# Pooled attention before two mixture-of-experts layers: K loaded in runs of 96 rows, a reordered start, and a routing carry on GpSimd

## The chip, the core and the metric

The program runs on one core of a Trainium2 chip. The metric is device time of one execution, in microseconds (us). The engines: TensorE (PE) for matmuls and transposes, VectorE (DVE), ScalarE (ACT), GpSimd (POOL), and SyncE (SP), whose queue issues nearly all loads and stores. Each engine runs its own instructions in the order in which they are written; waits between engines are semaphores.

## What is computed

```python
def _attn_ref(q, k, v):                       # 8 batches, 8 heads, 576 rows, 64 wide
    k_p = k.reshape(B, H, Sp, 8, D).mean(axis=3)      # 576 rows pooled to 72
    v_p = v.reshape(B, H, Sp, 8, D).mean(axis=3)
    scores = scale * np.matmul(q, k_p.transpose(0, 1, 3, 2))
    attn = softmax(scores)
    return np.matmul(attn, v_p)

x = attention, as 4608 tokens of 512
x = moe(x, ...)      # 8 experts, 512 -> 1024 -> 512, the best expert by x @ w_gate + modality bias
x = moe2(x, ...)     # the same with a skip score, added to x
```

## The kernel before

**Columns and units.** The attention stage works in 36 columns of 128 query rows. Two batches make nine columns: a unit is 256 rows of one batch (two columns, even and odd rows), and a ninth column holds the last 64 rows of both batches. For column c the engines do, in the loop from line 562: `emit_S` (TensorE: the scores, L310, into one PSUM tile of two banks that each column uses again; VectorE: their maximum `mx`, L316), `emit_qT` for column c + 2 (TensorE transposes q, L289; ScalarE copies it, L293), `emit_eT` for column c - 1 (L357, L359), `emit_exp` (TensorE subtracts the maximum with a matmul on `mx`, L336; ScalarE takes the exponential, L340), and `emit_AV` for column c - 3 (L377). `after_AV` then lets VectorE divide (`rec`, `x`, L395 to L402) and form the routing logits `LG` (L406); ScalarE and SP finish and store the unit's tokens to `xd`. S(c) below means the L310 matmuls of column c.

**Supply.** `load_q` brings a unit of q, `split_q` copies it on ScalarE (L167) three or four columns ahead of use. K and V are summed over eight rows: V of a batch in two halves of three runs of 96 rows (`load_v`, `pool_v`), the first half on GpSimd as three additions (L181 to L183), the second on VectorE as three reductions (L176). K of the first two batches comes in runs of 126 rows (`load_kb`, `pool_kb`, `prep_kb`); K of the other six in four tiles of 108 pooled rows that cross batches, each in two halves of four heads, summed on GpSimd (`load_k`, `pool_k`), transposed by `prep_k` (L239, four transposes) and copied to `KB` by ScalarE (L244). The tables `pool_at` and `prep_at` say in which column each sum and each preparation is issued; `order` and `free_after` say in which column a load is issued, as soon as the buffer three loads back is free. Instructions of VectorE in `pool_at` and the V scale `VB` (L260) are put into the list `late` and issued right behind the next column's `mx`.

**Routing beside the columns.** At columns 12, 21 and 30 a generator `route` is put into a background queue for nine columns each; every `bg.tick()` issues one step, six ticks a column, `pace` times (2 from column 22). The steps: `rt_mx` (VectorE, L838), three steps on `rt_eq` (GpSimd for the first two groups, L840 to L844), `lag[0]` idle steps, `rt_my` (VectorE, L850), `M` and `rt_ms` (GpSimd), `lag[1]` idle steps, a running sum `rt_i` (VectorE, L867), the carry to the next group (L871), a matmul, and the ranks `BB` (L891 to L901). Behind it in the same queue stand 18 one-hot tables `OB` (`route_places`, GpSimd, L911) for each group, then the next group's `route`. `count` (L916) sums the carry over partitions from a bfloat16 copy `cb`.

Of the kernel before, what the change touches and what calls it, by code (L numbers as in the profile page):

```python
# [9 lines left out]
F32 = mybir.dt.float32  # L10
# [26 lines left out]
NB0 = 2  # L37
KT = (B - NB0) * SP // 4
TILES = [(NB0 * SP + KT * i, NB0 * SP + KT * i + KT) for i in range(4)]

KR = [(126 * i, min(126 * i + 126, H * SP)) for i in range(5)]
VC = 96


def segments(t):

    g0, end = TILES[t]
    g = g0
    while g < end:
        b, sp = divmod(g, SP)  # L50
        n = min(SP - sp, end - g)
        yield b, sp, sp + n, g - g0
        g += n


def attention(tc, g, q, k, v, mid, w_gate, bias, const, moe):
# [4 lines left out]
    with ExitStack() as ctx:  # L61
# [55 lines left out]
        def load_k(t, hf):  # L117
            a = raw.tile([128, 5, POOL * D], F32, tag="k", name="kt", bufs=3)[:, 0:4]
            for b, s0, s1, p0 in segments(t):
                for h in range(4):  # L120
                    nc.sync.dma_start(
                        out=a[p0:p0 + s1 - s0, h, :],
                        in_=k[b, 4 * hf + h, s0 * POOL:s1 * POOL, :].rearrange(
                            "(s r) d -> s (r d)", r=POOL),
                    )
            raw_t["k", t, hf] = a
# [68 lines left out]
        def pool_k(t, hf, eng):  # L195
            d = sums_of(("k", t), [KT, H, D])
            pool_rows(d[:, 4 * hf:4 * hf + 4, :], raw_t.pop(("k", t, hf))[0:KT], eng)

# [34 lines left out]
        def prep_k(t):  # L233
            bg.settle()
            n = KT
            ks = sum_t.pop(("k", t))
            ps = ps_m.tile([128, 4, 128], F32, tag="m", name="ps_k")
            for hp in range(4):
                nc.tensor.transpose(  # L239
                    ps[:, hp, 0:n], ks[:, 2 * hp:2 * hp + 2, :].rearrange("p h d -> p (h d)"),  # L240
                    g.ident[0:n, 0:n])
            for b, s0, s1, p0 in segments(t):
                for i in range(2):
                    nc.scalar.copy(  # L244
                        KB[b % NR][64 * i:64 * i + 64, :, SP * i + s0:SP * i + s1],
                        ps[64 * i:64 * i + 64, :, p0:p0 + s1 - s0])
# [176 lines left out]
        def idle():  # L423
            for _ in range(3):
# [5 lines left out]
        pool_at = {0: [(pool_kb, 1, 2, 4, P), (pool_kb, 1, 0, 2, V), (pool_kb, 1, 4, 5, V)],  # L430
                   1: [(pool_v, 1, 0, P)]}
# [5 lines left out]
        for b, cs in ((1, (3, 4, 4)), (2, (5, 6, 7)), (3, (10, 11, 12)), (4, (14, 15, 16)),  # L437
                      (5, (18, 19, 20)), (6, (20, 21, 22)), (7, (24, 25, 26))):
# [21 lines left out]
        kq += [((pool_k, t, hf), [(load_k, t, hf)]) for t in range(4) for hf in range(2)]  # L460
# [1635 lines left out]
```

## Time and profile before

| | us |
|---|---|
| median of 3 runs | 941.45 |
| lowest, highest | 939.84, 943.73 |
| the profiled execution | 939.02 |
| its span | 937.3 |
| TensorE busy in the span | 891.4 (95%) |
| VectorE, GpSimd, ScalarE busy | 703.4, 510.6, 368.0 |

Attention covers the first 200 us, beside which the first expert blocks begin at 185. A row of the timeline gives start, duration, engine, line, operation, tile written and read, and in brackets the idle time before it and what ended that. A row of the windows gives the stretch, then busy time (and instructions) of PE, PEld, DVE, ACT and POOL, the clock granted to TensorE (1.00 is 2.4 GHz, 0.50 is 1.2 GHz), the DMA engines' busy share and GB/s.

### The profile page before, as it was taken

Reading aid. Unit: us, or ns where it says so; the run is one execution under the profiler, and the core shown is the slowest. Engines: PE = TensorE matmul, PEld = TensorE weight load, DVE = VectorE, ACT = ScalarE, POOL = GpSimd, SP = SyncE. Lnnn points to the kernel's source line nnn. Section 1 sums busy time; section 2 is a strip of 40 time slices with the busy share of each in tenths; the row PEclk is TensorE's granted clock in tenths of the full one; section 3 lists DMA queues with packets and bytes.
Section 4 is the critical chain, followed back from the end, with each engine's and each line's share of the span. In section 5 each row is a group of like instructions: output and inputs, shape, how many; then the busy total and the mean of one; then the engine's idle time right before and its main releaser. Section 6 shows DMA issues by size and latency. Waiting matters only on the chain. (4 is left out here: it accounts for less than half of the span.)

```text
span 937.3 us, 19065 instructions
## 1 busy us (share of the span) xinstructions
PE 891.4 (95%) x6231; PEld 801.6 (86%) x6231; DVE 703.4 (75%) x1815; ACT 368.0 (39%) x727; POOL 510.6 (54%) x762
## 2 busy tenths in 40 slices
PE   8899989899999999998999979999999999999995
PEld 6799889888899999987999869999988988979983
DVE  5487787887778888889877898877665778687672
ACT  4466556552222222251222422213414556565551
POOL 5766597413246657665766557575653444445341
PEclk9799899999999999999999999999999999999997
DMA  9999965623222211442224521227125683661441
GB/s 235 220 251 254 259 195 170 194 71 113 69 68 84 74 40 56 148 149 67 81 83 132 174 79 64 75 74 252 57 68 160 208 249 104 224 225 36 133 141 44
DMA packets 86141, 126.07 MB, mean 135 GB/s; under 512 B 13192, under 2 KB 50104, under 8 KB 85866
## 3 DMA queue, kind: packets, MB, share of 16 engines
q1 hardware_dynamic: 75386, 96.68, 33.1%
q0 software_dynamic: 10608, 27.67, 9.7%
q8 instruction: 63, 1.03, 0.5%
q14 instruction: 84, 0.69, 0.3%
HBM read 182.09 MB, written 39.50 MB: 236 GB/s over the span
## 5 line engine op out<-in xcount | busy, mean ns | idle before, releaser
L1414 PE MATMUL ps_g<-xh,w1h 128*128 128x256 f32 x896 | 256.3, 286 | 3.8 <-DVE hl L1419 2.2
L1414 PE MATMUL ps_g<-xl,w1h 128*128 128x256 f32 x896 | 253.2, 283 | 2.2 <-DVE xl L1367 2.2
L1414 PE MATMUL ps_g<-xh,w1l 128*128 128x256 f32 x896 | 252.3, 282 | 0.0
L1744 DVE CUSTOM_DVE_ANT_0 hr<-x,W 128x512 bf16<-128x512 f32 x324 | 227.9, 703 | 19.1 <-DVEq L1343 6.3
L1463 PE MATMUL ps_g<-w2h,hh 128*128 128x512 f32 x464 | 190.5, 411 | 3.2 <-ACT w2h L1354 1.9
L1463 PE MATMUL ps_g<-w2h,hl 128*128 128x512 f32 x464 | 185.1, 399 | 7.0 <-DVE hl L1419 7.0
L1463 PE MATMUL ps_g<-w2l,hh 128*128 128x512 f32 x464 | 184.1, 397 | 0.0
L1414 PEld LDWEIGHTS ps_g<-xh,w1h 128*128 128x128 f32 x896 | 169.2, 189 | 8.4 <-DVE hl L1419 2.6
L1414 PEld LDWEIGHTS ps_g<-xl,w1h 128*128 128x128 f32 x896 | 168.8, 188 | 3.9 <-DVE xl L1367 3.0
L1414 PEld LDWEIGHTS ps_g<-xh,w1l 128*128 128x128 f32 x896 | 169.2, 189 | 0.0
L1418 ACT ACTIVATE hh<-ps_g 128x512 fp32r<-128x512 f32 (+1 forms) x116 | 67.7, 583 | 242.5 <-PE ps_g L1414 240.3
L1419 DVE SCALAR_TENSOR_TENSOR hl<-ps_g,hh 128x512 fp32r<-128x512 f32 (+1 forms) x116 | 77.6, 669 | 65.6 <-ACT hh L1418 42.1
L911 POOL TENSOR_SCALAR OB<-iota,BB,pay 128x128 bf16<-128x128 bf16 x126 | 109.9, 881 | 23.7 <-DVE BB L899 13.9
L1463 PEld LDWEIGHTS ps_g<-w2h,hl 128*128 128x128 f32 x464 | 87.8, 189 | 30.0 <-DVE hl L1419 8.9
L1463 PEld LDWEIGHTS ps_g<-w2h,hh 128*128 128x128 f32 x464 | 88.3, 190 | 21.3 <-issue 2.8
L1463 PEld LDWEIGHTS ps_g<-w2l,hh 128*128 128x128 f32 x464 | 88.3, 190 | 16.5
L1355 DVE TENSOR_TENSOR w2l<-w2r,w2h 128x512 fp32r<-128x512 f32 x112 | 75.4, 711 | 6.5 <-ACT w2h L1354 4.3
L1334 POOL TENSOR_TENSOR w1l<-w1r,w1h 128x512 fp32r<-128x512 f32 x35 | 45.3, 1314 | 56.2 <-ACT w1h L1331 56.0
L1710 POOL DMA_INDIRECT out_dram<-x,dsi x38 | 47.7, 1255 | 43.8 <-DMA out_dram<-x,dsi 15.7
L1354 ACT CAST w2h<-w2r 128x512 fp32r<-128x512 f32 x112 | 63.9, 617 | 0.1
L1331 ACT CAST w1h<-w1r 128x512 fp32r<-128x512 f32 x112 | 63.7, 620 | 0.4 <-ACT hh L1418 0.4
L1655 POOL DMA_INDIRECT out_dram<-o,o2i x21 | 23.9, 1137 | 72.0 <-DVE o L1653 45.2
(299 smaller groups left out, 1421.8 us busy)
## 6 DMA issues: line engine op xcount, KB each, us to landing
w1r<-in_moe_w_dram SPq DMA_DIRECT2D x128, 512.0 KB
w2r<-in_moe_w_dram SPq DMA_DIRECT2D x124, 512.0 KB
x2s<-x SPq DMA_DIRECT2D x19, 522.0 KB
v<-in_v_dram SPq DMA_DIRECT2D x48, 192.0 KB
xd<-x SPq DMA_DIRECT2D x16, 520.0 KB
q_sb<-in_q_dram SPq DMA_DIRECT2D x16, 512.0 KB
kt<-in_k_dram SPq DMA_DIRECT2D x32, 144.0 KB
x2s<-OBx SPq DMA_DIRECT2D x16, 261.0 KB
```

What stands on the lines that cost most here:

```text
L911: e.tensor_scalar(g.ob(c)[:, i, :], g.iota, r.BB[:, c:c + 1], r.pay[:, i, c:c + 1], ALU.is_equal, ALU.mult)
L1331: self.nc.scalar.copy(self.w1h[f], raw)
L1334: low() if late is None else late.append(low)
L1354: self.nc.scalar.copy(self.w2h[f], raw)
L1355: (eng or self.nc.vector).tensor_tensor(self.w2l[f], raw, self.w2h[f].bitcast(F32), ALU.subtract)
L1414: nc.tensor.matmul(out, lhsT=a[f][:, k, :], rhs=b[:, k, :], start=(n == 0), stop=(n == 11))
L1418: nc.scalar.activation(out=hh, in_=whole, func=ACTF.Relu)
L1419: nc.vector.scalar_tensor_tensor(hl, in0=whole, scalar=0.0, in1=hh.bitcast(F32), op0=ALU.max, op1=ALU.subtract)
L1463: nc.tensor.matmul(ps, lhsT=a[f][:, tt], rhs=b[f], start=(n == 0), stop=(n == 23))
L1655: nc.gpsimd.indirect_dma_start(out=self.out, out_offset=bass.IndirectOffsetOnAxis(ap=si, axis=0), in_=o, in_offset=None, bounds_check=NT - ...
L1710: self.nc.gpsimd.indirect_dma_start(out=self.out, out_offset=bass.IndirectOffsetOnAxis(ap=self.dsi[i % 2][:, t:t + 1], axis=0), in_=self.x ...
L1744: self.nc.vector.tensor_tensor_reduce(out=self.junk, in0=self.x2[i % 2][:, t, 0:DM], in1=self.W9[:, e, :], scale=1.0, scalar=0.0, op0=ALU. ...
```

## The change

K of batches 2 to 7 is loaded, summed and transposed batch by batch, in two halves of three runs of 96 rows as V is: 36 loads instead of 64, 12 sums of 96x768 on GpSimd instead of 8 of 108x1024, 18 transposes of 96 instead of 16 of 108. At the start the third and fourth columns are issued ahead of `prep_kb(1)`; q is loaded a unit sooner, and `split_q` copies it three columns ahead throughout. The idle steps of `route` are other numbers, its carry is a GpSimd instruction for the first two groups, and where `count` has `copy` set, ScalarE makes `cb`.

```diff
+        def load_k(b, hf):
+            a = raw.tile([128, 5, POOL * D], F32, tag="k", name="kt", bufs=3)[0:VC, 0:3]
+            for i in range(3):
+                r0 = 288 * hf + VC * i
+                nc.sync.dma_start(out=a[:, i:i + 1, :], in_=rows(k, b, r0, r0 + VC, 1))
+            raw_t["k", b, hf] = a
...
-        for t, c0 in enumerate((3, 8, 16, 23)):
-            pool_at[c0] = [(pool_k, t, 0, P)]
-            pool_at[c0 + 1] = [(pool_k, t, 1, P)]
+        for b, cs in ((2, (3, 4)), (3, (7, 8)), (4, (11, 12)), (5, (16, 17)), (6, (19, 21)),
+                      (7, (22, 24))):
+            for hf, c in enumerate(cs):
+                pool_at[c] = [(pool_k, b, hf, P)]
         for b, c0 in ((2, 6), (3, 10), (4, 13), (5, 18), (6, 20), (7, 24)):
             pool_at.setdefault(c0, []).append((pool_v, b, 0, P))
...
-        order = [("k", 0), ("v", 0), ("v", 1), ("k", 1), ("v", 2), ("v", 3), ("k", 2), ("k", 3),
...
+        order = [("k", 0), ("v", 0), ("v", 1), ("k", 1), ("v", 2), ("v", 3)]
+        for b in range(NB0, B):
+            order += [("k", 2 * b - 2), ("k", 2 * b - 1), ("v", 2 * b), ("v", 2 * b + 1)]
...
-            if c < NC:
-                next_q(cols[c][0] + (5 if c > 1 else 4))
+            if c == 0:
+                for n in (4, 5, 6):
+                    next_q(n)
+                    next_kv(0, 1)
+                next_kv(0)
+            elif c == 2:
                 next_kv(c)
-                next_q(cols[c][0] + 5)
+                next_q(7)
+            elif c < NC:
+                next_q(cols[c][0] + 6)
+                next_kv(c)
...
+            elif c == 2:
+                emit_S(c)
+                emit_eT(c - 1)
+                prep_v2(0)
+                emit_exp(c)
+                split_q(2)
+            elif c == 3:
+                emit_S(c)
+                emit_eT(c - 1)
+                emit_qT(4)
+                emit_exp(c)
+                prep_kb(1)
...
             emit_AV(c - LAG)
+            if c == 3:
+                emit_qT(5)
...
-            ahead = c + (3 if c < 2 else 4)
-            if ahead < NC and cols[ahead][0] not in qs_t:
+            ahead = c + 3
+            if ahead < NC and c > 2 and cols[ahead][0] not in qs_t:
                 split_q(cols[ahead][0])
...
-                eng, lag = (nc.vector, (0, 0)) if c0 == 18 else (nc.gpsimd, (5, 8) if c0 == 0 else (4, 12))
+                eng, lag = (nc.vector, (0, 0)) if c0 == 18 else (nc.gpsimd, (5, 1) if c0 == 0 else (6, 3))
...
-        V.tensor_copy(r.carry, I[:, :, n - 1])
+        eng.tensor_copy(r.carry, I[:, :, n - 1])
...
-        nc.vector.tensor_copy(cb, r.carry)
+        (nc.scalar.copy if copy else nc.vector.tensor_copy)(cb, r.carry)
```

**The start, on TensorE,** from the transposes of column 1's exponentials to S(4) (the first row on `KB_129`, the second batch's K). `ps_k` are the K transposes of `prep_kb(1)`, of which the first of nine is shown, `ps_g` is `prep_v2(0)`. Before:

```order
L357 MATMUL ps_et<-ident,ec 96x128 x6
L336 MATMUL ps_s<-mx,nident 128x288 x2
L289 MATMUL ps_q<-ident,qs 128x128 x4
L217 MATMUL ps_k<-ident,kb 64x126
...
L274 MATMUL ps_g<-WGV,vt 96x32 x3
L310 MATMUL ps_s<-KB_128,qt 128x144 x4
...
L377 MATMUL ps_av<-VB_134,et 128x146 x6
L310 MATMUL ps_s<-KB_129,qt 128x144 x4
```

Here S(3) stands behind the K transposes and `ps_g`. The same stretch on TensorE after:

```order
L338 MATMUL ps_et<-ident,ec 96x128 x6
L255 MATMUL ps_g<-WGV,vt 96x32 x3
L317 MATMUL ps_s<-mx,nident 128x288 x2
L291 MATMUL ps_s<-KB_128,qt 128x144 x4
...
L270 MATMUL ps_q<-ident,qs 128x128 x4
...
L199 MATMUL ps_k<-ident,kb 64x126
...
L358 MATMUL ps_av<-VB_134,et 128x146 x6
L270 MATMUL ps_q<-ident,qs 128x128 x4
L291 MATMUL ps_s<-KB_129,qt 128x144 x4
```

S(3), the last row on `KB_128`, has moved ahead of the nine K transposes and of the transposes of q for column 4.

**Between the first two routing groups, on GpSimd.** `OB` is written behind the first group's ranks `BB`; `rt_eq` reads the second group's `rt_mx`. `t` is the sum's first addition (two more follow each). Before:

```order
L911 TENSOR_SCALAR OB<-iota,BB_664,pay_666 128x128 x2
L181 TENSOR_TENSOR t_1536<-v 96x768
...
L911 TENSOR_SCALAR OB<-iota,BB_664,pay_666 128x128 x8
L181 TENSOR_TENSOR t_1673<-v 96x768
...
L840 TENSOR_TENSOR rt_eq<-LG,rt_mx 128x72
```

The 18 tables (the third piece is eight again) hold two V sums between them. The same place on GpSimd after:

```order
L913 TENSOR_SCALAR OB<-iota,BB_644,pay_646 128x128 x3
L163 TENSOR_TENSOR t_1469<-kt 96x768
...
L163 TENSOR_TENSOR t_1535<-v 96x768
...
L163 TENSOR_TENSOR t_1600<-kt 96x768
...
L163 TENSOR_TENSOR t_1676<-v 96x768
...
L163 TENSOR_TENSOR t_1740<-kt 96x768
...
L842 TENSOR_TENSOR rt_eq<-LG,rt_mx 128x72
```

Between the 18 tables stand five sums instead of two, and `rt_eq` stands behind all of them as before.

**The same place on VectorE.** The first group's `BB` stands in column 17 (before: 18), and the second group's `rt_my`, which reads GpSimd's `rt_eq`, in column 22 (before: 23). After, in column 22:

```order
L297 TENSOR_REDUCE mx<-ps_s 128x8
L241 TENSOR_TENSOR VB_139<-v,half 96x12x64
L158 TENSOR_REDUCE v<-v 96x64
L840 TENSOR_REDUCE rt_mx<-LG 128x9
L387 TENSOR_REDUCE LG<-lg 128x8
L852 TENSOR_REDUCE rt_my<-rt_eq 128x9
```

`rt_my` now follows `rt_mx` in the same column, with one instruction between them, and column 23's `mx` stands behind it.

## Rows read from the trace of the kernel before

**Rows 1.** Windows: the start, and the stretch around column 17

```profile
20.00:40.00 20.00, 15.15 (x85) 12.17 (x84) 5.41 (x10) 7.81 (x16) 13.70 (x15) 0.74 0.90 226
...
92.00:108.00 16.00, 14.06 (x97) 13.42 (x98) 11.41 (x26) 7.74 (x17) 6.19 (x6) 0.79 0.99 272
```

**Rows 2.** Timeline of TensorE at the start, columns 2 to 5

```profile
24.95 0.51 PE L336 MATMUL ps_s<-mx,nident 128*128 128x288 f32 x2 [2.15 <-DVE mx L316]
26.68 1.12 PE L289 MATMUL ps_q<-ident,qs 128*128 128x128 f32 x4 [1.22 <-ACT qs L167]
27.59 0.42 PE L217 MATMUL ps_k<-ident,kb 126*64 126x126 f32 x1
...
31.29 0.45 PE L222 MATMUL ps_k<-ident,kb 72*64 72x72 f32 x2
...
37.62 1.66 PE L377 MATMUL ps_av<-VB,et 96*128 96x146 f32 x12
39.12 1.15 PE L310 MATMUL ps_s<-KB,qt 128*128 128x144 f32 x8
40.10 0.60 PE L289 MATMUL ps_q<-ident,qs 128*128 128x128 f32 x4
...
43.14 1.14 PE L310 MATMUL ps_s<-KB,qt 128*128 128x144 f32 x8
```

**Rows 3.** Timeline of VectorE: the last piece of the second batch's K

```profile
23.21 1.02 DVE L176 TENSOR_REDUCE kb<-kb 72x64 f32<-72x512 f32 x1 [1.88 <-DMA kb<-in_k_dram]
```

**Rows 4.** Timeline of ScalarE: copies of q that waited for their load

```profile
25.58 1.04 ACT L167 COPY qs<-q_sb 128x1024 f32<-128x1024 f32 x1 [4.68 <-DMA q_sb<-in_q_dram]
...
93.77 1.05 ACT L167 COPY qs<-q_sb 128x1024 f32<-128x1024 f32 x1 [0.25 <-DMA q_sb<-in_q_dram]
```

**Rows 5.** Timeline of VectorE: running sum and carry in column 16, running sum in column 32

```profile
92.92 2.37 DVE L867 TENSOR_TENSOR_SCAN rt_i<-within,rt_ms 128x72 bf16<-128x72 f32 x1
95.33 1.18 DVE L871 CAST carry<-rt_i 128x8 f32<-128x8 bf16 x1
...
169.15 0.31 DVE L867 TENSOR_TENSOR_SCAN rt_i<-within,rt_ms 128x72 bf16<-128x72 f32 x1
```

**Rows 6.** Timeline of GpSimd beside the first running sum: two additions of a K sum

```profile
92.76 2.37 POOL L181 TENSOR_TENSOR t<-kt 108x1024 f32<-108x1024 f32 x1
95.20 1.27 POOL L182 TENSOR_TENSOR t<-t 108x512 f32<-108x512 f32 x1
```

**Rows 7.** Timeline of TensorE: S(17), the wait behind it, S(18), S(19), S(24), a wait, S(26)

```profile
93.85 1.20 PE L310 MATMUL ps_s<-KB,qt 128*64 128x144 f32 x16
...
98.39 0.85 PE L336 MATMUL ps_s<-mx,nident 128*128 128x288 f32 x2 [1.94 <-DVE mx L316]
...
102.43 2.18 PE L310 MATMUL ps_s<-KB,qt 128*128 128x144 f32 x8
...
108.02 1.23 PE L310 MATMUL ps_s<-KB,qt 128*128 128x144 f32 x8
...
129.00 1.14 PE L310 MATMUL ps_s<-KB,qt 128*128 128x144 f32 x8
...
132.25 0.51 PE L336 MATMUL ps_s<-mx,nident 128*128 128x288 f32 x2 [1.02 <-DVE mx L316]
...
141.66 1.20 PE L310 MATMUL ps_s<-KB,qt 128*64 128x144 f32 x16
```

**Rows 8.** Timeline of GpSimd behind the first ranks: one V sum's start, tables

```profile
108.50 1.80 POOL L181 TENSOR_TENSOR t<-v 96x768 f32<-96x768 f32 x1
...
112.03 6.20 POOL L911 TENSOR_SCALAR OB<-iota,BB,pay 128x128 bf16<-128x128 bf16 x8
...
121.76 6.97 POOL L911 TENSOR_SCALAR OB<-iota,BB,pay 128x128 bf16<-128x128 bf16 x8
```

**Rows 9.** Timeline of VectorE: the first group's ranks, the second group's rt_my

```profile
106.66 0.17 DVE L899 CAST BB<-rt_ri 128x9 f32<-128x9 int32 x1
...
129.95 0.23 DVE L850 TENSOR_REDUCE rt_my<-rt_eq 128x9 f32<-128x72 f32 x1 [1.74 <-POOL rt_eq L844]
```

More of the change, by code (lines that the diff above doesn't have):

```diff
@@ L37 @@
 NB0 = 2
-KT = (B - NB0) * SP // 4
-TILES = [(NB0 * SP + KT * i, NB0 * SP + KT * i + KT) for i in range(4)]
 KR = [(126 * i, min(126 * i + 126, H * SP)) for i in range(5)]
 VC = 96
[L45 to L53, printed above, removed]
 def attention(tc, g, q, k, v, mid, w_gate, bias, const, moe):
@@ L115, in load_kb @@
                 nc.sync.dma_start(out=a[0:n, i:i + 1, :], in_=rows(k, b, *KR[i], 1))
[L117 to L126, printed above, removed]
+        def load_k(b, hf):
[4 more added lines that the diff above has]
+            raw_t["k", b, hf] = a
         def load_v(b, hf):
@@ L231, in prep_kb, with prep_k @@
             copy(KBb[64:128, 3, SP:2 * SP], ps[64:128, 0:SP])
-        def prep_k(t):
+        def prep_k(b):
             bg.settle()
[L235 to L243, printed above, removed]
+            ks = sum_t.pop(("k", b))
+            ps = ps_m.tile([128, 4 * SP], F32, tag="m", name="ps_k")
+            for i in range(3):
+                nc.tensor.transpose(ps[:, VC * i:VC * i + VC],
+                                    ks[:, i].rearrange("p g d -> p (g d)"), g.ident[0:VC, 0:VC])
+            for i in range(2):
+                view = ps[64 * i:64 * i + 64].rearrange("p (h s) -> p h s", s=SP)
+                for r in range(2):
                     nc.scalar.copy(
-                        KB[b % NR][64 * i:64 * i + 64, :, SP * i + s0:SP * i + s1],
-                        ps[64 * i:64 * i + 64, :, p0:p0 + s1 - s0])
+                        KB[b % NR][64 * r:64 * r + 64, 2 * i:2 * i + 2, SP * r:SP * r + SP],
+                        view[:, r::2, :])
         vt_t = {}
@@ L429, in attention @@
         P, V = nc.gpsimd, nc.vector
[L430 to L434 removed]
+        pool_at = {0: [(pool_kb, 1, 2, 4, P), (pool_kb, 1, 0, 2, V)],
+                   1: [(pool_v, 1, 0, P), (pool_kb, 1, 4, 5, V)]}
+        for b, cs in ((2, (3, 4)), (3, (7, 8)), (4, (11, 12)), (5, (16, 17)), (6, (19, 21)),
+                      (7, (22, 24))):
+            for hf, c in enumerate(cs):
+                pool_at[c] = [(pool_k, b, hf, P)]
         for b, c0 in ((2, 6), (3, 10), (4, 13), (5, 18), (6, 20), (7, 24)):
             pool_at.setdefault(c0, []).append((pool_v, b, 0, P))
[L437 removed]
+        for b, cs in ((1, (3, 4, 4)), (2, (6, 7, 8)), (3, (10, 11, 12)), (4, (14, 15, 16)),
                       (5, (18, 19, 20)), (6, (20, 21, 22)), (7, (24, 25, 26))):
@@ L459, in attention @@
               for b in range(NB0)]
-        kq += [((pool_k, t, hf), [(load_k, t, hf)]) for t in range(4) for hf in range(2)]
+        kq += [((pool_k, b, hf), [(load_k, b, hf)]) for b in range(NB0, B) for hf in range(2)]
         vq = [((pool_v, b, hf), [(load_v, b, hf)]) for b in range(B) for hf in range(2)]
-        order = [("k", 0), ("v", 0), ("v", 1), ("k", 1), ("v", 2), ("v", 3), ("k", 2), ("k", 3),
-                 ("v", 4), ("v", 5), ("k", 4), ("k", 5), ("v", 6), ("v", 7), ("v", 8), ("v", 9),
-                 ("k", 6), ("k", 7), ("v", 10), ("v", 11), ("k", 8), ("v", 12), ("v", 13), ("k", 9),
-                 ("v", 14), ("v", 15)]
+        order = [("k", 0), ("v", 0), ("v", 1), ("k", 1), ("v", 2), ("v", 3)]
+        for b in range(NB0, B):
+            order += [("k", 2 * b - 2), ("k", 2 * b - 1), ("v", 2 * b), ("v", 2 * b + 1)]
         at = []
@@ L569, in attention @@
                 emit_S(c, lambda: emit_qT(c + 2))
-            elif c < 4:
+            elif c < 2:
                 if c > 0:
```

18 lines of the change are left out of this document (9 added, 9 removed).

## The prediction

> **What bounds the kernel now.** I read the windows first, then TensorE's own waits in the timeline, then what VectorE and GpSimd do at those places. TensorE is busy through nearly all of attention, and so are VectorE and the DMA engines; what a change can win is where TensorE stops or runs at 1.2 GHz. Two windows show that: the start, with a granted clock of 0.74 over 20 us, and the stretch around column 17, with 0.79 over 16 us [rows 1]. At half speed stood therefore 2 x 0.26 x 20 = 10.4 us and 2 x 0.21 x 16 = 6.7 us, which cost 5.2 and 3.4 us of work. Both falls come behind waits: 2.15 us for `mx` of column 2 and 1.22 us for a copy of q [rows 2], and 1.94 us for `mx` of column 17 [rows 7]. Elsewhere a column takes 4.2 us: from S(19) at 108.02 to S(24) at 129.00 are five [rows 7]. Behind attention the expert blocks go from engine to engine with TensorE as the bound, so I pass a shift of attention's end on to the end of the program one to one.
>
> **Start: 6.5 us won.** In column 2, VectorE held `mx` back behind the last piece of K, whose load came at 23.21 [rows 3]; now that piece stands behind `mx`. The next fixed event is the load of q's third unit, at 25.58 [rows 4]: all loads issued ahead of it are the same in the same order, so I leave it there. From it: copy 1.04, to 26.6; transposes for column 4, 0.60, to 27.2; maximum of column 3, 0.5, to 27.7. The nine K transposes took from 27.59 to 31.74 at half clock [rows 2], 2.1 at full: 29.8. AV(0) holds TensorE 1.5 (37.62 to 39.12), under which ScalarE copies K; transposes for column 5, 0.60; S(4) at 31.9 instead of 39.12. Then TensorE waits once more, since the q of column 6 is copied only now (the copy of column 5's transposes, taken as 0.6 like the transposes, then 1.04: 33.5), and from those transposes to the next S are 3.0 (40.10 to 43.14): S(5) at 36.5 to 36.6 instead of 43.14. The pauses left there are 0.8, 0.4 and 1.0 us, spread over 10; I take the clock as staying at 2.4 GHz. Bounds: 7.2 won (S(4) alone), 1.3 if it falls as before (S(5) 5.2 later).
>
> **Column 17: 5.8 us won.** From S(17) at 93.85 to S(19) at 108.02 are 14.2 us for two columns of 4.2 [rows 7]. The cause is VectorE: running sum 2.37, carry 1.18 [rows 5]. Both end with a GpSimd instruction: the sum ends at 95.29, GpSimd's addition at 95.13; the carry at 96.51, the next addition at 96.47 [rows 6]. In column 32, where GpSimd stands idle, the same running sum takes 0.31 [rows 5]. After the change GpSimd waits for the running sum in order to write the carry, so no addition is under way: 0.31 and no carry on VectorE. The 3.2 us that this frees are more than the wait of 1.94, and without the wait the clock doesn't fall.
>
> The Trainium skill, "SBUF — State Buffer", section "Who interferes with whom", has the rule: a VectorE instruction with two SBUF inputs, or in a 2-port mode, and a GpSimd instruction that reads SBUF exclude each other for the whole instruction, and the earlier one goes first; the two rows agree. It also speaks against this change, which fills GpSimd without a pause from column 17 to 22, beside two V scales of VectorE. The trace shows such a case: eight tables took 6.97 us beside one and 6.20 without [rows 8]; by the rule either engine can lose up to an instruction (1.8 us) at each scale, and the result would be, as an estimate, 1 to 3 us later than mine.
>
> **Columns 22 and 23: 15 us lost.** GpSimd works in order, and VectorE's `rt_my` waits for `rt_eq`, which stands behind all tables of the first group. Before, from `BB` at 106.66 to `rt_my` GpSimd did 18 tables and two sums without a pause, and VectorE waited 1.74 us [rows 9], TensorE 1.02 [rows 7]. After, five columns lie between the two again (17 to 22 instead of 18 to 23), with the same tables but five sums: the second half of K of batch 5 and both of batch 6 have come between. One sum of 96 rows is 3.53 us (108.50 to 112.03) [rows 8]; K's have the same shape. So VectorE waits 1.74 + 3 x 3.53 = 12.3 us. Behind it stand column 22's divisions and `mx` of column 23, and behind that TensorE, ScalarE, everything. TensorE loses 0.7 less, as before: 11.6. Then it runs at half clock; the nearest row is the fall behind 1.94 us in column 17, 3.4 us; the start's 5.2 is the upper bound, 2 the lower (a stretch in which part of the work waits anyway). Sum 15.0, bounds 12.5 to 17.5. SP's loads of K for batch 7 wait behind GpSimd's sums and hold back stores and q behind them; those have ten columns (q) and six (the four token tiles) in hand.
>
> **Columns 24 and 25: 3.3 us won.** S(24) to S(26) took 12.7 us, 4.3 too many [rows 7]: the wait of `rt_my` (counted above in its new place), the second group's running sum and carry beside GpSimd, and K of tile 3 arriving late. All three go. I give 1.0 back, since about ten small VectorE steps of the routing now fall into one column with a V scale and a V sum; 2 and 4.3 are the ends.
>
> **At no cost.** K's 18 transposes of 96 instead of 16 of 108 are the same columns; ScalarE's eight more small copies lie in its pauses (it is busy 15.6 us of the 36 in the two windows of [rows 1]); 28 fewer loads only help SP; the casts of `cb` that move to ScalarE have eight elements each.
>
> **Sum.** -6.5 - 5.8 + 15.0 - 3.3 = -0.6 us. The profiled execution took 939.0, 2.4 below the median: 938.4 for it, 940.9 for the median. A measurement of this kernel tells about 0.5%, 4.7 us, from no change.
>
> **Rivals.**
> *The backlog doesn't bind:* the sums of K end early enough, or `rt_my` comes late enough, that VectorE doesn't wait. It would need GpSimd to do 33 us of work in the 22 between; for it speaks only that GpSimd is busy 510.6 us of the span of 937.3, so has room on average. Then 15 us are not lost: 926. Decides if the wait of `rt_my` is under 2 us. Chance 0.12.
> *The start stays at half clock (slower):* TensorE pauses three times between 23 and 34 us, and the clock falls near 26 as before. Half clock for the 10.4 us of before takes 5.2 us: S(5) at 41.8, result 946. It decides if the pauses of TensorE from 23 to 27 us sum to nearly the 3.4 of before instead of my 1.2; against it speaks that no pause there is above 1 us. Chance 0.20.
> *Loads become the bound:* from column 5 to 22 TensorE runs 6 to 12 us ahead of before while the DMA engines are at 0.99 of their time around column 17 [rows 1], and a copy of q waited for its load even before [rows 4]. Against it: q is now loaded a unit (8.4 us) sooner and copied a column later, and K has bigger pieces. If it binds, about 3 us before column 17 are lost: 944. Chance 0.13.
>
> **How the numbers follow.** The forecast has 0.55; its own spread, from the ends above, is about 4 us either way. Faster by over 0.5%: the first rival and the forecast's lower end, 0.12 + 0.08 = 0.20. Slower: half of the second rival, a quarter of the third, the forecast's upper end, 0.10 + 0.03 + 0.09 = 0.22. Within: 0.58. The range 934 to 949 takes in the forecast with its ends and the two later rivals, and leaves out the first.
>
> **What would show it.** S(5) at 36 to 37 us with the clock at 1.00 from 20 to 40; the running sum near 0.3 us and no wait at column 17, S(19) near 96; then one wait of TensorE for `mx` of 11 to 12.5 us near 115 to 127, VectorE waiting for `rt_eq`, GpSimd without a pause ahead of it, and a granted clock of 0.5 for some 7 us behind it; S(26) and S(27) within 2 us of before. If that wait is absent the forecast is wrong towards 926; if the start shows 0.74 again, towards 946.

## The result: 0.7% slower, and where the profile shows it

The changed kernel took 947.5 us in the median of 12 runs (943.9 to 949.8), the kernel before 940.8 beside it (12 runs, 937.6 to 943.7). The ratio is 1.0073, with a 95% interval of 1.0058 to 1.0089: 6.7 us slower, a little more than the 0.5% that this measurement can tell from no change. The forecast was 940.9, no change. The time lies inside the range; the sign was missed.

The profiled execution of after took 949.8 us (span 948.1), that of before 939.0 (span 937.3). The spans differ by 10.8 us, more than the medians: this execution of after lies 2.3 above its median, that of before 1.8 below its own.

Start of the scores in each column, S(c), in us, and how far after is ahead (-) or behind (+):

| | before | after | difference |
|---|---|---|---|
| S(5) | 43.14 | 37.20 | -5.9 |
| S(10) | 64.72 | 58.40 | -6.3 |
| S(11) | 68.65 | 64.13 | -4.5 |
| S(17) | 93.85 | 89.65 | -4.2 |
| S(19) | 108.02 | 98.24 | -9.8 |
| S(22) | 120.75 | 110.86 | -9.9 |
| S(24) | 129.00 | 134.49 | +5.5 |
| S(27) | 146.31 | 150.80 | +4.5 |
| S(33) | 173.83 | 178.15 | +4.3 |
| last AV matmuls | 197.31 | 204.82 | +7.5 |
| end of the span | 937.3 | 948.1 | +10.8 |

Windows of after: stretch, then busy us (and instructions) of PE, PEld, DVE, ACT and POOL, the granted clock, the DMA engines' share, GB/s. The first and third answer to [rows 1].

```profile
20.00:40.00 20.00, 17.54 (x136) 15.56 (x137) 11.35 (x19) 12.15 (x24) 13.25 (x15) 1.00 1.10 233
40.00:92.00 52.00, 50.70 (x449) 48.73 (x448) 40.48 (x100) 34.12 (x80) 39.82 (x62) 1.00 1.07 287
92.00:108.00 16.00, 16.00 (x146) 15.44 (x146) 12.86 (x32) 11.25 (x27) 14.60 (x16) 1.00 0.98 265
108.00:128.00 20.00, 9.70 (x83) 9.21 (x81) 7.62 (x18) 6.35 (x14) 19.01 (x23) 0.85 0.78 211
128.00:142.00 14.00, 11.28 (x60) 10.81 (x61) 7.26 (x20) 5.05 (x13) 10.94 (x13) 0.61 0.26 76
185.00:205.00 20.00, 19.21 (x139) 18.23 (x140) 12.50 (x44) 7.63 (x20) 3.93 (x6) 0.83 0.31 121
```

The start and column 17 now run at full clock. The loss stands in 108 to 142: TensorE has work for 9.70 of 20 us and then runs at half clock, while GpSimd is busy for 19.01 of those 20. A second fall of the clock, 0.83, stands at 185 to 205, where the kernel before had 1.00.

TensorE in after, answering to [rows 2] and [rows 7]: S(3), S(4), S(5); a wait in column 10; S(17) to S(19); the wait of column 23 and what follows it; S(24), S(25), S(27); the AV matmuls that ran at half clock much later.

```profile
25.59 1.25 PE L291 MATMUL ps_s<-KB,qt 128*128 128x144 f32 x8 [0.79 <-ACT ec L321]
...
32.53 1.15 PE L291 MATMUL ps_s<-KB,qt 128*128 128x144 f32 x8
...
37.20 1.14 PE L291 MATMUL ps_s<-KB,qt 128*128 128x144 f32 x8
...
61.83 0.51 PE L317 MATMUL ps_s<-mx,nident 128*128 128x288 f32 x2 [1.16 <-DVE mx L297]
...
89.65 1.20 PE L291 MATMUL ps_s<-KB,qt 128*64 128x144 f32 x16
...
93.92 1.17 PE L291 MATMUL ps_s<-KB,qt 128*128 128x144 f32 x8
...
98.24 1.23 PE L291 MATMUL ps_s<-KB,qt 128*128 128x144 f32 x8
...
129.34 0.85 PE L317 MATMUL ps_s<-mx,nident 128*128 128x288 f32 x2 [11.51 <-DVE mx L297]
129.97 3.13 PE L358 MATMUL ps_av<-VB,et 96*128 96x146 f32 x12
134.49 2.29 PE L291 MATMUL ps_s<-KB,qt 128*128 128x144 f32 x8 [1.39 <-ACT ec L321]
...
140.84 1.17 PE L291 MATMUL ps_s<-KB,qt 128*128 128x144 f32 x8
...
150.80 1.23 PE L291 MATMUL ps_s<-KB,qt 128*128 128x144 f32 x8
...
186.76 3.13 PE L358 MATMUL ps_av<-VB,et 96*128 96x146 f32 x12
```

The 11.51 us are the wait that the prediction put there. New is the wait behind it, 1.39 us for ScalarE's exponential. What made these waits, on GpSimd, VectorE and ScalarE in that order (GpSimd's lines answer to [rows 8], VectorE's to [rows 9]):

```profile
93.08 2.38 POOL L913 TENSOR_SCALAR OB<-iota,BB,pay 128x128 bf16<-128x128 bf16 x3 [4.69 <-DVE BB L901]
95.43 1.81 POOL L163 TENSOR_TENSOR t<-kt 96x768 f32<-96x768 f32 x1
...
125.42 0.58 POOL L165 TENSOR_TENSOR k<-t 96x192 f32<-96x192 f32 x1
125.96 0.31 POOL L842 TENSOR_TENSOR rt_eq<-LG,rt_mx 128x72 f32<-128x72 f32 x1
...
132.77 0.19 POOL L873 CAST carry<-rt_i 128x8 f32<-128x8 bf16 x1 [0.41 <-DVE rt_i L869]
```

```profile
127.22 0.23 DVE L852 TENSOR_REDUCE rt_my<-rt_eq 128x9 f32<-128x72 f32 x1 [12.24 <-POOL rt_eq L846]
...
132.40 0.31 DVE L869 TENSOR_TENSOR_SCAN rt_i<-within,rt_ms 128x72 bf16<-128x72 f32 x1 [1.83 <-POOL rt_ms L865]
```

```profile
133.00 0.20 ACT L922 CAST rc_cb<-carry 128x8 bf16<-128x8 f32 x1 [15.21 <-POOL carry L873]
133.10 0.79 ACT L340 COPY et<-ps_et 96x768 f32<-96x768 f32 x1
133.79 0.65 ACT L321 ACTIVATE ec<-ps_s 128x576 f32<-128x576 f32 x1
```

From `BB` to `rt_my` GpSimd works without a pause: 18 one-hot tables (`OB`) and five sums, 93.08 to 127.2. The last three rows are the part that the prediction didn't have. The cast `rc_cb`, 0.20 us long, was moved to ScalarE; there it stands ahead of the copy `et` and of column 23's exponential, and it waits for a carry that comes from GpSimd only at 132.8. TensorE had done with column 23's scores at about 130.2 (129.34 and 0.85); the exponential began at 133.79.

### The profile page after: what moved, and what is told of

It reads as the page before. It is cut to its first block, busy times and chain, and to the rows that moved or that the text cites. A ratio compares the mean times of both kernels' runs of the same rounds, so it can differ in the third digit from the quotient of the medians.

```text
span 948.1 us, 19056 instructions
## 1 busy us (share of the span) xinstructions
PE 892.2 (94%) x6233; PEld 802.6 (85%) x6233; DVE 700.5 (74%) x1810; ACT 369.5 (39%) x738; POOL 518.7 (55%) x776
## 3 DMA queue, kind: packets, MB, share of 16 engines
q8 instruction: 63, 1.03, 0.5%
## 5 line engine op out<-in xcount | busy, mean ns | idle before, releaser
L358 PE MATMUL ps_av<-VB,et 96*128 96x146 f32 (+1 forms) x480 | 63.1, 296 | 0.0
```

The source lines that it names most:

```text
L358: nc.tensor.matmul(ps[p0:p1, j // 3, o:o + 2 * VW], lhsT=t[:, j, p0:p1], rhs=VB[b % NR][:, j].rearrange("p i w -> p (i w)"), start=(j % 3 ...
```

## The experiments

Each median is of 5 to 12 runs; the ratio is to the kernel before on the same chip, with its 95% interval. S(22), S(27) and the last AV matmuls are from one profiled execution each.

| kernel | S(22) | S(27) | last AV | median | ratio to before |
|---|---|---|---|---|---|
| before | 120.8 | 146.3 | 197.3 | 939.2 to 940.8 | |
| after | 110.9 | 150.8 | 204.8 | 947.5 | 1.0073 (1.0058 to 1.0089) |
| after, once more | 108.9 | 148.7 | 202.7 | 947.6 | 1.0077 (1.0049 to 1.0104) |
| after, cast on VectorE | 109.9 | 147.7 | 198.5 | 942.1 | 1.0020 (1.0004 to 1.0036) |
| after, carry copy on VectorE | 109.9 | 152.7 | 203.6 | 948.3 | 1.0102 (1.0080 to 1.0124) |
| start alone | 114.6 | 147.6 | 198.7 | 939.2 | 0.9984 (0.9965 to 1.0002) |
| start and routing, no K runs | 115.4 | 151.4 | 202.1 | 944.0 | 1.0020 (0.9997 to 1.0043) |
| routing alone | 117.5 | 151.2 | 203.6 | 942.9 | 1.0028 (1.0012 to 1.0044) |
| K runs alone | 114.9 | 148.9 | 199.7 | 943.0 | 1.0033 (1.0019 to 1.0046) |
| after, first tables on VectorE | 115.4 | 145.3 | 196.2 | 942.6 | 1.0024 (1.0005 to 1.0044) |
| after, first tables later | 111.2 | 141.4 | 193.9 | 936.6 | 0.9966 (0.9946 to 0.9985) |
| the same, cast on VectorE | 111.0 | 141.9 | 192.8 | 935.2 | 0.9951 (0.9932 to 0.9970) |
| the same, scan later | 110.4 | 136.8 | 194.7 | 937.2 | 0.9979 (0.9961 to 0.9997) |
| the same, second tables shared | 114.7 | 142.9 | 197.4 | 933.6 | 0.9941 (0.9923 to 0.9958) |

**The cast alone.** The changed kernel with `rc_cb` back on VectorE:

```diff
-        (nc.scalar.copy if copy else nc.vector.tensor_copy)(cb, r.carry)
+        nc.vector.tensor_copy(cb, r.carry)
```

> The changed kernel with the bfloat16 cast of the carry (rc_cb) back on VectorE; all else stays. In the changed kernel the cast on ScalarE waited 15.21 us for GpSimd's carry and stood ahead of the copy and the exponential of column 23, whose matmul had been done at 129.3 and which began only at 133.8. Theory A: without it the exponential of column 23 begins 1 to 3 us earlier, the scores matmul of column 24 at 132 to 133.5 instead of 134.5, and the median falls by 1 to 2 us to 945.5 to 946.5. Rival: the wait for the carry only changes its engine (VectorE now waits there, and stands ahead of rec and x), column 24 stays at 134 to 135, and the median stays at 947 to 948.

ScalarE's exponential of column 23, VectorE's cast and S(24) of that run:

```profile
129.27 0.65 ACT L321 ACTIVATE ec<-ps_s 128x576 f32<-128x576 f32 x1 [11.62 <-PE ps_s L317]
```

```profile
132.00 1.75 DVE L922 CAST rc_cb<-carry 128x8 bf16<-128x8 f32 x1 [0.29 <-POOL carry L873]
```

```profile
131.90 2.13 PE L291 MATMUL ps_s<-KB,qt 128*128 128x144 f32 x8
```

The exponential waits for nothing but its matmul. S(24) comes 2.6 us sooner than in after and S(27) 3.1; 1.0 of each was there already at S(23), a difference of the start between executions, so the cast cost 1.6 us at S(24) and 2.1 at S(27). The half clock behind TensorE's wait was shorter, too: 6.3 us past the end of that wait, in after 9.6. The first window is of this run, the second of after; the next window of each stands at 1.00 again.

```profile
128.30:134.60 6.30, 6.26 (x26) 6.25 (x27) 4.12 (x9) 0.83 (x3) 5.50 (x9) 0.50 0.56 168
```

```profile
129.30:138.90 9.60, 8.18 (x34) 7.71 (x35) 4.23 (x12) 2.28 (x7) 8.65 (x12) 0.50 0.37 109
```

The 12.2 us wait at `rt_my` stays. The median fell by more, from 947.5 to 942.1: in this run's profile the second fall of the clock is absent too (window 185 to 205 at 1.00), worth 3.2 us at the last AV matmuls. Theory A, with a larger effect than expected (the exponential 4.5 us sooner instead of 1 to 3, the median 5.4 instead of 1 to 2).

**After, once more**, to see what belongs to the change and what to one execution.

> The changed kernel once more, unaltered, beside the variants. In its first profile TensorE ran at half clock twice, in columns 23 to 25 and again from 187 to 193, and the second time cost 3 us that the profile of the kernel before doesn't have. Theory A (the 11.5 us of idle TensorE bring the first stretch, the second is chance): VectorE's wait of 12.2 us and the half clock of columns 23 to 25 are there again, column 27 at 150 to 151.5, the second stretch is absent or as long; median 946 to 949. Rival (the second stretch belongs to the change): half clock from 185 to 195 again, with a loss of 2 to 3 us between columns 33 and 35.

The wait at `rt_my` is 12.21 us and TensorE's 11.47, as in the first profile, though this execution was 2.0 us further ahead from S(11) on; for the same reason S(27) came at 148.7 and not at 150 to 151.5. The second fall is there again:

```profile
184.72 3.13 PE L358 MATMUL ps_av<-VB,et 96*128 96x146 f32 x12
```

AV takes 3.13 us instead of 1.66, and S(33) to S(35) 11.7 us against 10.2 in before. That looks like the rival, but over all fourteen profiles S(33) to S(35) is either 10.2 us (before and seven others) or 11.7 to 11.8 (after twice, routing alone, and three of the kernels below, with the cast on either engine). The wait of 2.2 us for VectorE ahead of it is there in before too. So it is not tied to one edit; what starts it stays open.

**The start alone**: the kernel before with the new order of the start and q sooner; as in the change, the V sums and V preparation of the third batch come a column later. Everything else is old.

```diff
-            ahead = c + (3 if c < 2 else 4)
+            ahead = c + 3
...
+            elif c == 3:
+                emit_S(c)
+                emit_eT(c - 1)
+                emit_qT(4)
+                emit_exp(c)
+                prep_kb(1)
```

> The kernel before with the new start alone (queries loaded a unit sooner and copied three columns ahead, fourth column ahead of the second K): K in its old tiles, old lags, carry and cast on VectorE. Theory A: the scores matmul of column 5 at 36 to 38 instead of 43.1 with a granted clock of 1.00 from 20 to 40, and, if the lead is passed on, column 27 near 140.5 and the median 934 to 936 (941 less 5.9). Rival (the lead meets something that does not move with TensorE): GpSimd's sums and transfers keep their own time, the wait of column 17 grows from 2 us by as much, column 27 stays at 145 to 146.5, the median at 939 to 942.

S(5) came at 37.55, 5.6 us ahead of before, at full clock. The lead then shrank to 1.6 at S(16), first by a wait of 1.4 us for a K sum in column 8, and the stall of column 17 was shorter (S(17) to S(18) 5.2 us instead of 8.6). At S(22) the front was 6.2 us ahead, and lost all of that and more in one place, VectorE first, TensorE behind it:

```profile
119.86 1.02 DVE L176 TENSOR_REDUCE v<-v 96x64 f32<-96x512 f32 x1 [6.51 <-DMA v<-in_v_dram]
```

```profile
122.39 1.12 PE L289 MATMUL ps_q<-ident,qs 128*128 128x128 f32 x4 [6.68 <-ACT qs L167]
```

Here the V transfer ended the wait, not `rt_eq`. The time is the rival's, 939.2; its place was not column 17 but columns 22 and 23, and S(27) came at 147.6, behind the rival's 145 to 146.5. From this run on I held another theory: a front that comes early meets a wall at column 22, whatever made it early. For transfers this run and the next bear it out; for GpSimd's work the runs show something else, as the account below has it.

**Start and routing together**, the change without the K runs:

```diff
-        V.tensor_copy(r.carry, I[:, :, n - 1])
+        eng.tensor_copy(r.carry, I[:, :, n - 1])
```

(with the new lags, the cast on ScalarE and the start above).

> The changed kernel without the K loads in runs of 96: the kernel before with the new start, carry on GpSimd, cast on ScalarE and the new lags. Theory A (three more K sums ahead of the second group make the backlog): no wait of VectorE at rt_my above 4 us, column 27 at 134 to 137, median 929 to 933 (941 less 5.9 for the start and 5.8 for column 17). Rival (the lead itself makes the backlog: an engine that runs 10 us ahead of GpSimd's 16 sums and 18 one-hot writes meets them whatever form K has): VectorE waits 8 to 12 us at rt_my also here, column 27 at 143 to 147, median 938 to 943.

S(22) was 5.4 us ahead, then VectorE waited 4.9 us for V and TensorE 5.1 for a copy of q; S(27) was 5.1 behind. The loss is the rival's in kind, somewhat larger (944.0 against 938 to 943, S(27) 151.4 against 143 to 147), but again by transfers, with 1.2 us at `rt_my`. The prediction's step that takes the lead through to the end fails without any K runs.

**Routing alone**: the kernel before with carry, cast and lags of the change.

> The kernel before with the routing part of the change alone: carry on GpSimd, its cast on ScalarE, the new lags; old start, K in old tiles. Theory A (the prediction's step): the stall of column 17 goes (scores of column 19 near 102.5 instead of 108.0), and the 5.5 to 5.8 us are passed on: column 27 near 140.5, median 934 to 936. Theory B (two limits at one place, formed on the runs with the new start): an engine that is ahead meets, with K in old tiles, the transfers in columns 21 to 23, where VectorE waited 6.5 us for V and TensorE 6.7 us for qs; the lead is given back there, column 27 at 145 to 148, median 939 to 943.

Column 17's stall went as expected (S(17) to S(19) 8.6 us instead of 14.2), and S(22) was 3.3 us ahead. Then VectorE waited 3.8 us at `rt_my`, TensorE 5.1, and ScalarE stood at the cast:

```profile
130.94 0.20 ACT L920 CAST rc_cb<-carry 128x8 bf16<-128x8 f32 x1 [6.79 <-POOL carry L871]
```

S(27) was 4.9 us late, at 151.2 (theory B: 145 to 148). Theory B's time; the releaser was GpSimd, not V. With the new lag `BB` stands in column 17, so that the K sum of that column is behind it: three sums between `BB` and `rt_my` instead of two.

**K runs alone**: the kernel before with K's loads, sums and transposes of the change.

> The kernel before with K in runs of 96 rows alone (its loads, sums, transposes and their columns); old start, carry and cast on VectorE, old lags. Theory B: transfers move more in the same time (287 instead of 247 GB/s from 40 to 92 in the changed kernel), so they bind nowhere; GpSimd's sums and one-hot writes meet an engine front that is 10 us later than in the changed kernel, so VectorE waits 0 to 6 us at rt_my instead of 12.2; column 27 at 144 to 149, median 938 to 943. Rival (the prediction's term, three more sums ahead of the second group cost 12 to 15 us wherever TensorE stands): VectorE waits 10 to 14 us at rt_my, column 27 at 156 to 161, median 951 to 957.

```profile
131.32 0.23 DVE L831 TENSOR_REDUCE rt_my<-rt_eq 128x9 f32<-128x72 f32 x1 [8.20 <-POOL rt_eq L825]
```

From 40 to 92 us 271 GB/s were moved, against 245 to 247 in the four kernels with K in tiles and 287 in after. S(22) was 5.9 us ahead of before, and the wait was 6.5 longer than the 1.74 of [rows 9]: neither 0 to 6 nor 10 to 14. S(27), 148.9, and the time, 943.0, are theory B's. The rival counted three more sums, but here `BB` stands in column 18 as in before, with the sum of column 17 ahead of it, and only two more sums lie between `BB` and `rt_my`. At the prediction's 3.53 us each that makes 1.74 + 7.06 = 8.8, and 8.2 were measured.

**After, first tables on VectorE**, so that GpSimd has 14 us less in front of `rt_eq`:

```diff
-                places = route_places(tc, g, g.r1, c0, n, nc.gpsimd, nc.vector if c0 == 18 else None)
+                places = route_places(tc, g, g.r1, c0, n, nc.vector if c0 == 0 else nc.gpsimd,
+                                      nc.vector if c0 == 18 else None)
```

> The changed kernel with one thing moved: the first group's 18 one-hot writes (OB, 0.78 us each on GpSimd in the changed kernel's trace, about 14 us) go to VectorE, where the third group's take 0.31 us each (5.5 us). Theory A (GpSimd's backlog is what the change lost): VectorE's wait of 12.24 us at rt_my and TensorE's of 11.51 us behind it fall below 2 us, the half clock behind them goes, the scores matmul of column 27 comes at 137 to 143 instead of 150.8, and the median falls from 947.5 to 932 to 940. Theory B (the K loads in runs of 96 are what costs, through transfers): the wait only changes its releaser to a transfer of K or V, column 27 stays at 149 to 151, and the time stays within 944 to 949. Theory C (VectorE has no room): the waits go, but the 5.5 us on VectorE are paid in full in columns 18 to 22, column 27 near 146, time 942 to 944.

The wait at `rt_my` fell to 1.1 us. But the tables on VectorE, first beside a sum on GpSimd, then with GpSimd idle:

```profile
93.59 2.58 DVE L914 TENSOR_SCALAR OB<-iota,BB,pay 128x128 bf16<-128x128 bf16 x3
...
99.21 0.75 DVE L914 TENSOR_SCALAR OB<-iota,BB,pay 128x128 bf16<-128x128 bf16 x3
```

0.86 us each against 0.25. S(18) to S(22) took 22.6 us instead of 16.9 in after. S(27) at 145.3 and 942.6 us are nearest to theory C: the work was moved to the engine that TensorE waits for.

**After, first tables later**: same engine, same work, behind the second group's ranks.

```diff
-                if c0 < 18:
-                    bg.add(places)
+                if c0 == 0:
+                    held = places
+                if c0 == 9:
+                    bg.add(held)
+                    bg.add(places)
```

> The changed kernel with the first group's 18 one-hot writes put behind the second group's ranks (same engine, same work, later). Theory B: GpSimd has 14 us less ahead of the second group's rt_eq and VectorE gets nothing more to do, so the waits of 12.2 and 11.5 us fall below 2, column 27 comes at 135 to 140 and the median at 931 to 938. Rival (a third limit stands at the same place: transfers of V, or GpSimd's 36 one-hot writes, 28 us, that now stand between column 25 and the first gather): the front stalls again in columns 21 to 26 or the gather comes late, column 27 at 143 to 149, median 940 to 946.

`rt_my` came at 116.4 instead of 127.2, and the cast on ScalarE still held up S(24):

```profile
116.42 0.23 DVE L855 TENSOR_REDUCE rt_my<-rt_eq 128x9 f32<-128x72 f32 x1 [1.13 <-POOL rt_eq L849]
```

```profile
122.18 0.20 ACT L925 CAST rc_cb<-carry 128x8 bf16<-128x8 f32 x1 [4.07 <-POOL carry L876]
```

```profile
123.68 2.29 PE L291 MATMUL ps_s<-KB,qt 128*128 128x144 f32 x8 [3.13 <-ACT ec L321]
```

936.6 us, 10.9 below after, by one move. This is the run that shows that the 18 tables in front of `rt_my` decided: the K runs, the start and the carry are all still in it. S(27) and the time miss the expected ranges narrowly or not at all (141.4 against 135 to 140; 936.6 in 931 to 938).

**The same with the cast on VectorE.**

> The changed kernel with the first group's one-hot writes behind the second group's ranks and the cast rc_cb back on VectorE. Theory B: as with the one-hot writes moved alone, and ScalarE's exponential no longer stands behind the cast: column 27 at 135 to 138, median 930 to 936, 0 to 3 us below the run without the cast moved. Rival (third limit): column 27 at 142 to 147, median 938 to 943.

935.2 us, theory B's time; the 1.4 us to the run before lie inside the intervals of both. S(27) came at 141.9 and not at 135 to 138. The cast is now the VectorE instruction that lies beside a sum, and TensorE waits for it; then the clock falls:

```profile
124.30 0.17 PE L929 MATMUL R<-rc_cb,ones 128*128 128x8 bf16 x1 [2.05 <-DVE rc_cb L925]
```

```profile
124.00:128.00 4.00, 2.73 (x15) 2.48 (x15) 3.80 (x10) 1.90 (x6) 3.77 (x5) 0.64 0.52 164
```

**The same with the second group's scan later** (lag 9 instead of 3).

> The changed kernel with the first group's one-hot writes behind the second group's ranks, the cast rc_cb on VectorE, and the second group's scan three quarters of a column later (lag 9 instead of 3). In the run without the later scan VectorE waited 1.8 us for rt_ms, which stood behind a K sum, its cast took 1.75 us beside that sum, TensorE waited 2.05 us for it and then ran at half clock from 124 to 132, columns 24 to 25 taking 9.5 us. Theory B: with the scan behind the max of column 24 rt_ms is there, no wait of VectorE above 0.5 us, columns 24 to 25 in 4.5 to 6 us, column 27 at 137 to 139.5, median 931 to 934. Rival (half clock comes anyway, from the shorter waits of columns 22 and 23): column 27 at 141 to 142.5, median 934.5 to 937.

S(27) at 136.8, 9.5 us ahead of before, and no fall of the clock up to there. But the cast still took 1.75 us, S(24) to S(25) 7.1 (4.5 to 6 expected), and 937.2 us is no gain: the lead met the same engine again behind S(30), where the matmuls `W` read the one-hot tables. The tables of both groups, 36, now stand in one row on GpSimd.

```profile
130.03 28.34 POOL L916 TENSOR_SCALAR OB<-iota,BB,pay 128x128 bf16<-128x128 bf16 x36
```

```profile
158.43 0.19 PE L1037 MATMUL W<-er_oa,OB 128*128 128x2 bf16 x1 [0.59 <-POOL OB L916]
```

This is the last of four such waits, 2.1 us in sum (the 7 us written ahead of the next run are not in the trace); behind them the clock was at 0.5 (window 158.4 to 165.1: 0.58). S(30) to S(32) took 14.2 us instead of 8.8.

**The same with every second table of the second group on VectorE.**

> The run with the later scan, and of the second group's 18 one-hot writes every second one on VectorE. In the run before, GpSimd wrote 24 one-hots in a row from 139.4 to 158.4 (0.79 us each), and TensorE waited 7 us in column 30 for the last of them (the matmuls of W), then ran 8 us at half clock: the lead of 9.5 us at column 27 was 3.1 at column 32. Theory B (GpSimd's one-hot writes are the limit that the front meets next): with 9 of them on VectorE, where 0.3 to 0.8 us each are paid in columns 28 to 30, GpSimd is through by 152, TensorE doesn't wait for OB, column 32 comes at 158.5 to 161 instead of 165.1 (before: 168.2), and the median is 930 to 934. Rival (the end of attention isn't passed on, since the gathered tokens or the weights of the experts set the start of the expert part): column 32 at 158.5 to 161 but the median at 935 to 939.

```profile
133.61 21.33 POOL L916 TENSOR_SCALAR OB<-iota,BB,pay 128x128 bf16<-128x128 bf16 x27
```

```profile
161.74 1.04 PE L1037 MATMUL W<-er_oa,OB 128*128 128x2 bf16 x36
```

No wait for a table, S(30) to S(32) 8.8 us as in before. The median is 933.6 us, within the expected range and the lowest of all: 0.59% below before and 14 us below after. It is clear of the run before it, not of the one with the cast on VectorE alone (0.9923 to 0.9958 against 0.9932 to 0.9970). Its profiled execution was a late one from the start (S(18) at 96.4, 262 GB/s from 40 to 92), so that S(32), 166.6, is no test of the expected 158.5 to 161.

**The carry's copy back on VectorE**, the rest as in after.

> The changed kernel with the copy of the carry back on VectorE (the cast stays on ScalarE, the lags as in the changed kernel). Theory B (the stall of column 17 in the kernel before was the meeting of scan and carry with a sum on GpSimd at that moment, not the carry's engine): column 17 to 18 takes 4.3 to 5.3 us, the copy 0.2 to 1.2 us; the wait at rt_my stays at 11 to 13 us; median 945 to 949. Theory A (the prediction's step, the carry's engine decides): the stall of column 17 to 18 comes back, 8 to 9 us, the front is 4 us later there and the wait at rt_my as much shorter (7 to 9 us), median 946 to 949, so the time alone doesn't tell them apart and column 18 does: 93.5 to 95 against 97.5 to 99.

```profile
83.01 0.94 DVE L869 TENSOR_TENSOR_SCAN rt_i<-within,rt_ms 128x72 bf16<-128x72 f32 x1
83.99 0.90 DVE L873 CAST carry<-rt_i 128x8 f32<-128x8 bf16 x1
```

Column 17's stall doesn't come back: S(17) to S(18) 4.3 us, S(18) at 93.0 (93.5 to 95 expected). The two still end with GpSimd's additions (83.79 and 84.87), but the scan met only the end of one, and 2.37 + 1.18 us [rows 5] have become 1.84. With the start alone and with K runs alone, too, where scan and carry both stay on VectorE, most of that stall was gone (5.2 and 4.5 us). So moving the carry is one way to lose it and not the only one. The second group paid: its carry copy on VectorE ended at 134.25, the cast on ScalarE behind it waited 17.4 us, and S(27) came 1.9 us later than in after.

## Why the prediction missed, step by step

**The sum against what was measured**, up to S(27), from the table of columns:

| step | predicted | measured | how |
|---|---|---|---|
| start | -6.5 | -5.9 | S(5) |
| columns 6 to 22 (column 17) | -5.8 | -3.9 | -9.9 at S(22) less -5.9 |
| columns 22, 23 (backlog) | +15.0 | +15.4 | S(22) to S(24): 23.63 against 8.25 |
| columns 24 to 26 (forecast: 24, 25) | -3.3 | -1.0 | S(24) to S(27): 16.31 against 17.31 |
| sum at S(27) | -0.6 | +4.5 | |

The half clock and the cast's cost lie on both sides of S(24), so the rows on columns 22 to 26 can be held against the forecast only together: +14.4 against +11.7. In the run with the cast on VectorE they are +12.3 (S(22) to S(27): 37.84 against 25.56).

**Right.** The start at full clock with S(5) at 37.2 (36.5 to 36.6 forecast); the rivals of the start and of the loads didn't come, and GpSimd's backlog bound. The wait of `rt_my` came at 12.24 us (12.3 forecast), TensorE's at 11.51 (11.6), the half clock behind it (window 128 to 142 at 0.61) for 9.6 us where some 7 were forecast. The bounds of that term, 12.5 to 17.5, are wider than its own parts give: 11.6 with 2 and with 5.2 are 13.6 and 16.8. Column 17's stall is gone. The end of attention is passed on: from the last AV matmuls to the end of the span the fourteen profiled executions take 739.5 to 744.2 us, with 740.0 in before.

**Failed: "at no cost", the cast.** The prediction counted the cast's eight elements and not its place. On ScalarE it stands ahead of the exponential and waits for GpSimd, 15.21 us, the last 2.8 of them (130.2 to 133.0) with column 23's scores ready. It has shown 2.1 us at S(27), most of the 2.7 by which columns 22 to 26 came out above the forecast, and the run without it has a median 5.4 lower, with intervals that don't meet (1.0058 to 1.0089, 1.0004 to 1.0036). With that run at 942.1, 1.3 above before, the forecast would have held within its own spread. So the move of the cast makes the difference; the profiles tie 2.1 us of it to the wait, and how the other 3.3 arise is not shown. The second fall of the clock would give about 3: both profiles of after have it and the one without the cast has not, and the mean granted clock of whole executions was 0.976 to 0.982 in the twelve of after and 0.982 to 0.988 in the twelve without. But other kernels have that fall or not with the cast on either engine. With the first tables later, where the cast waited 4.07 us, the same move made no clear difference.

**Failed: columns 6 to 22, 1.9 us short.** Column 10 lost 1.8 us of lead, S(10) to S(11) 5.7 us instead of 3.9. Between the `mx` of columns 9 and 10 VectorE has the token set-up, and now a sum of V as well: the change issues the V sums of batch 2 in columns 6 to 8 instead of 5 to 7, which the prediction left out.

```profile
56.17 1.04 DVE L158 TENSOR_REDUCE v<-v 96x64 f32<-96x512 f32 x1
...
57.57 1.18 DVE L815 TENSOR_SCALAR ti<-tm,qf 128x4 int32<-128x4 f32 x1
...
59.00 0.86 DVE L820 CAST pay<-th 128x36 f32<-128x36 int32 x1
```

In before that sum came a column earlier, at 58.05, and the set-up took 2.3 us instead of 2.8, beside other work of GpSimd (0.33 and 1.14 us for the two instructions of it shown). `mx` came late and TensorE waited the 1.16 us shown above. In the kernels with the old start, which have V's old columns too, this column takes 3.9, with the new one 4.8 to 6.6; no run moves that sum alone.

**Right in size and in kind: the backlog.** GpSimd's work from `BB`, which lets the first table start, to `rt_my` has a length of its own: 23.3 us with 18 tables and two sums (before), 30.2 with four sums (K runs alone), 34.4 with five (after, and the three other executions with the same five). VectorE comes to `rt_my` 21.5 to 22.2 us behind `BB` in all of them, and the rest is wait: 1.74, 8.20, 12.21 to 12.24. So each further sum is paid, as the prediction had it. My theory during the experiments, that the wait grows by what the front has gained, does not hold here: after once more was 2.0 us ahead of after, its `BB` came 2.0 sooner, and the wait stayed the same. `BB` in after, then `BB` and `rt_my` in after once more, then `BB` in K runs alone:

```profile
92.81 0.16 DVE L901 CAST BB<-rt_ri 128x9 f32<-128x9 int32 x1
```

```profile
90.84 0.16 DVE L901 CAST BB<-rt_ri 128x9 f32<-128x9 int32 x1
...
125.22 0.23 DVE L852 TENSOR_REDUCE rt_my<-rt_eq 128x9 f32<-128x72 f32 x1 [12.21 <-POOL rt_eq L846]
```

```profile
101.16 0.17 DVE L880 CAST BB<-rt_ri 128x9 f32<-128x9 int32 x1
```

The three parts of the change each gained 3 to 6 us by S(22) and none kept them at S(27), for two reasons: more sums behind `BB` (K runs alone, routing alone), or, with K in tiles and the new start, a V transfer whose wait ended at 119.1 and 119.9 us. In the whole change it is the sums. With the first tables put behind the ranks, 14 us less stand in that stretch, the wait is 1.13 us and the lead gets through: -5.0 at S(27) instead of +4.5, and 10.9 us in the median.

**The rule weighed ahead of the result.** The prediction cited the Trainium skill, "SBUF — State Buffer", section "Who interferes with whom", against the change: V scales of VectorE beside a GpSimd without pauses, 1 to 3 us. The case came, and cost TensorE nothing: V's scale at 95.81, beside an addition from 95.43 to 97.24, took 2.24 us in after against 0.94 at 112.74, and S(18) to S(19) took 4.3. The same rule agrees with the tables of 0.86 against 0.25 us and with the cast of 1.75 against 0.17 (at 135.45 in before); those did reach TensorE. A scale can lose that time, as the estimate had it (1.3 of up to 1.8 us), but the slack behind it decided.

**From S(27) to 6.7 us.** The second fall of the clock added 3.0 to the +4.5 by the last AV matmuls (+7.5), the rest of the program took 743.3 us instead of 740.0, and the two profiled executions lie 2.3 above and 1.8 below their medians: 7.5 + 3.3 - 2.3 - 1.8 = 6.7.

## What to carry to other kernels

For an engine that works in order, add up what stands between the instruction that lets it start and the one that others wait for, and hold it against the time that the front needs between the same two. Work that comes into that stretch is paid even if the front is early (three sums, 11 us, here); work taken out of it lets earlier edits pay. A load that doesn't move with the front ends a lead as well. An instruction that is given to another engine takes its wait along: ask what is queued behind it there, however few elements it has. Put-off work comes back at its reader: after the wait of column 22 was gone, the same tables made one behind S(30).

## What the runs showed of the hardware

- With K in runs of 96 rows instead of pieces of 72 and 36 more is moved in the same time: 271 to 298 GB/s from 40 to 92 us in the kernels at hand that have it, but for one execution at 262, against 245 to 247 in the four without. The Trainium skill, "DMA: Bandwidth & Descriptors", section "Why a DMA increments its semaphore by 16 and not by 1", says that a transfer is spread over the largest number of engines up to 16 that divides its outer dimension: 16 for 96 rows and, worked out from that rule, 12 for 72 and 36. The trace agrees in the direction: the engines' mean share rose from 0.94 to 1.07. No run here varies the row count alone.
- Small VectorE instructions that began beside a GpSimd addition ended with it: the cast of 128x8 took 1.75 us (132.00 to 133.75, the addition 131.93 to 133.73), the set-up of 128x4 1.18, a table of 128x128 0.86 in the mean of three. The same cast took 0.17 us where it began ahead of the addition (135.45 and 135.47 in before). Reductions beside the same sums keep their 1.03 us.
- The granted clock fell to 0.5 within TensorE's wait of 11.5 us and stayed there to 138.9, 9.6 us past its end (S(24) 2.29 us, S(25) 1.17). It also fell behind a wait of 2.2 us near column 34 in six of the fourteen profiles, and did not in the other eight behind the same wait; each fall cost 1.6 us by S(35) and up to 3.2 by the last AV matmuls.
